# Which engine issues the stores of x: SyncE's queue or ScalarE's

## The chip, the cores and the metric

The kernel runs on one core of a Trainium2 chip. The metric is the time of one execution on the device, in microseconds (us). The engines are TensorE (PE; its weight loads are shown as PEld), VectorE (DVE), ScalarE (ACT), GpSimd (POOL) and SyncE (SP). Each has a queue of instructions that it works through in order; SP computes nothing and issues most of the DMA transfers.

## The reference

The program is attention followed by two mixtures of experts. All inputs are float32.

```
q, k, v: [4, 8, 576, 64]          # batch, heads, positions, head dim
out = upsample4(softmax_attention(mean4(q), mean4(k), mean4(v)))   # 144 pooled positions
    + softmax_attention(q, k, v, masked to |i - j| < 4)            # a local band
x  = out as rows [2304, 512]

# first mixture: 8 experts, two per row, the choice is made on noisy logits
logits = x @ w_gate + softplus(x @ w_noise) * noise
x  = sum over the two best e of  softmax weight * relu(x @ w1[e]) @ w2[e]      # w1 512x1024, w2 1024x512

# second mixture: 8 experts, one per row
logits = x @ w_gate2 + modality_bias[modality_id]
out = softmax probability of the best e * relu(x @ w1'[e]) @ w2'[e]
```

## The kernel before

**Attention.** The 32 heads are handled in pairs; one pair of one batch is a block, numbered 0 to 15, and two blocks make a group that shares its loads. The loop at L1114 is a software pipeline over the blocks: in one turn i it transposes q and k of block i+1, scores block i, and finishes the softmax, the transposes of the probabilities (`p_transposes`) and the product with v for blocks i−1 and i−2. The result of a batch lies transposed in `xT`.

**The rows x.** The 2304 rows are 18 tiles of 128 rows (t = 0 to 17). `xback_att(t)` turns a tile back to rows: PE multiplies pieces of xT with an identity that has the two routers' gate columns beside it (L971), into a PSUM tile px. What reads px is put off: a function `rest` is kept in the list `after`, and the next `flush()` runs it, so that PE isn't followed at once by work that waits for it. `rest` copies x from px to the SBUF tile `xr` on ACT (L987), sums the logits on DVE (L988) and stores xr into the DRAM rows `x_rows` (L989). xr has two buffers, so the copy of tile t must wait until the store of tile t−2 has landed. Tiles 0 to 12 are made inside the loop (the tables `before` and `behind` say in which turn); tiles 13 to 17 follow in a loop of their own (L1184), which I call the tail.

**Loads.** SP issues, in program order, the loads of q and k (`load_qk`, ten DMAs for a group), of v in two layouts (`load_vr`, two; `load_vw`, five), the small tables, two fills with zeros (`x_rows` beyond the 2304 rows at L1173; all of `x2_rows` at L1181), the routing weights `wb` (L1030), and the expert weights `raw` (L694 and L695, two DMAs of 512 KB for each). `ffn.begin` (L1176) issues the first two blocks of raw during turn 14, just ahead of the zeros of x2_rows; raw has three buffers, and the third block is loaded in the first step of `ffn.run`.

**Routing.** The first router's work (`route1`) is a generator. Its steps on DVE, POOL and PE are taken a few at a time between the instructions of attention (`tick`), from turn 12 on. When the places of the first tokens are known, POOL gathers their rows from x_rows (L720).

**Expert layers.** `FFN.run` goes through 20 items of up to 640 rows. An item's rows are gathered, transposed (L729), and multiplied in float32 split into a high and a low part (L746, L758); ACT and DVE split the weights (L706 to L709).

The order is written out by hand: the program is under a manual schedule, and each engine's queue has the instructions in the order of the code. The change touches L989 alone.

Of the kernel before, what the change touches and what calls it, by code (L numbers as in the profile page):

```python
# [871 lines left out]
def core(ctx, tc, q, k, v, moe_w_gate, moe_w_noise, moe_noise, moe_w1, moe_w2,  # L872
         moe2_modality_id, moe2_w_gate, moe2_modality_bias, moe2_w1, moe2_w2, out):
    nc = tc.nc
    B, H, S, D = q.shape
    DM = H * D
# [9 lines left out]
    x_rows = dram.tile([N + 640, XW], F32, tag="x_rows", name="x_rows")  # L886
# [28 lines left out]
    with ExitStack() as actx:  # L915
# [51 lines left out]
        def xback(t, halves):  # L967

            for o, b, s, n in pieces(t):
                for j in range(4):  # L970
                    nc.tensor.matmul(halves[j // 2][o:o + n, j % 2], att.xT[b][:, j, s:s + n], gw[:, j], start=True, stop=True)  # L971
            xr = axr.tile([128, 2, 2, 128], F32, tag="xr", name="xr")
            return xr
# [7 lines left out]
        def xback_att(t):  # L981
            px = att.psD.tile([128, 2, 512], F32, tag="D", name="px")
            pv = px[:, :, :2 * XB].rearrange("p a (b c) -> p a b c", b=2)
            xr = xback(t, [pv[:, 0], pv[:, 1]])

            def rest():
                nc.scalar.activation(xr, pv[:, :, :, :128], AF.Copy)  # L987
                nc.vector.tensor_reduce(lg[:, t], pv[:, :, :, 128:].rearrange("p a b c -> p c a b"), axis=AX.XY, op=ALU.add)  # L988
                nc.sync.dma_start(x_rows[128 * t:128 * t + 128, :DM], xr.rearrange("p a b c -> p (a b c)"))  # L989
            after.append(rest)  # L990

        def route1(c0, c1, bank, eng, heng, then=None):
# [203 lines left out]
    for i in range(5):  # L1196
        t = fpool.tile([128, YW], F32, tag=f"y{i}", name=f"y{i}")
# [473 lines left out]
```

## Time and profile before

Three runs took 926.56 to 929.01 us, with a median of 927.85. One more execution was profiled; the rows below come from it.

| | |
|---|---|
| profiled execution | 926.93 us |
| its span, first to last instruction | 925.2 us |
| PE busy | 870.4 us (94%) |
| DVE, ACT, POOL busy | 550.4, 429.0, 322.3 us |
| mean granted TensorE clock | 0.973 |
| stores of xr | 18 of 256 KB, all on SP |

How to read it: busy shares are averages over the stages. Attention lasts to about 178 us of the span, the expert layers from there to the end, and the two have different limits. DMA-issuing instructions aren't counted as busy time; in the timeline they stand under the queue's name (SPq), and their duration is the time until the queue can go on, not until the data has landed. A granted clock of 1.00 is 2.4 GHz, 0.50 is 1.2 GHz.

### The profile page before, as it was taken

To read this page: it belongs to the slowest core of one execution; us is meant where nothing else is said; L and a number is where in the kernel's file an instruction comes from. 1 tells how busy PE (TensorE), PEld (TensorE's weight loads), DVE (VectorE), ACT (ScalarE), POOL (GpSimd) and SP (SyncE) were. 2 spreads that over 40 slices of the span, in tenths; PEclk is the share of its full clock that TensorE was granted. 3 is DMA by queue.
4 is the path that set the end of the run, shared out by engine and by line. 5 is a ranking of instruction groups with operands and counts; after the bars stand their busy time and mean duration, and the time that the engine had idled before them with its cause. 6 is when DMAs were issued, how large, how long until landed. Compare 5 with 4: busy or idle time off the path is not lost. (4 is left out here: it accounts for less than half of the span.)

```text
span 925.2 us, 18236 instructions
## 1 busy us (share of the span) xinstructions
PE 870.4 (94%) x6775; PEld 764.1 (83%) x6775; DVE 550.4 (59%) x1345; ACT 429.0 (46%) x947; POOL 322.3 (35%) x460
## 2 busy tenths in 40 slices
PE   5898977799999999999999999989989999999995
PEld 4777866698888988999898999978867889999994
DVE  6775697489975544554343443434666877556662
ACT  3675644455554534444233342334423356455552
POOL 7876658436553213043106032050020442222210
PEclk9998988899999999999999999999989999999998
DMA  8878659747776457476328245175433467546650
GB/s 175 171 159 189 169 143 329 240 167 229 204 235 195 140 146 181 143 204 147 129 71 182 92 92 162 46 161 161 128 99 109 155 239 245 190 154 220 216 209 24
DMA packets 158702, 153.83 MB, mean 166 GB/s; under 512 B 74319, under 2 KB 119887, under 8 KB 158608
## 3 DMA queue, kind: packets, MB, share of 16 engines
q1 hardware_dynamic: 146528, 120.15, 42.2%
q0 software_dynamic: 12080, 32.45, 15.2%
q8 instruction: 56, 0.92, 0.4%
q14 instruction: 38, 0.31, 0.1%
HBM read 124.98 MB, written 27.85 MB: 165 GB/s over the span
## 5 line engine op out<-in xcount | busy, mean ns | idle before, releaser
L746 PE MATMUL ph<-xh,whi 128*128 128x256 f32 (+3 forms) x768 | 238.4, 310 | 2.8 <-DVE wlo L707 2.1
L746 PE MATMUL ph<-xl,whi 128*128 128x256 f32 (+3 forms) x768 | 237.6, 309 | 0.4 <-DVE xl L732 0.3
L746 PE MATMUL ph<-xh,wlo 128*128 128x256 f32 (+3 forms) x768 | 237.6, 309 | 0.1
L758 PE MATMUL y<-whi,hh 128*128 128x512 f32 x472 | 192.2, 407 | 0.1
L758 PE MATMUL y<-wlo,hh 128*128 128x512 f32 x472 | 188.1, 398 | 0.0
L758 PE MATMUL y<-whi,hl 128*128 128x512 f32 x472 | 187.6, 398 | 0.0
L707 DVE TENSOR_TENSOR wlo<-raw,whi 128x512 fp32r<-128x512 f32 x135 | 93.2, 690 | 157.4 <-ACT whi L706 144.9
L706 ACT ACTIVATE whi<-raw 128x512 fp32r<-128x512 f32 x160 | 101.0, 631 | 170.7 <-PE y L758 155.7
L746 PEld LDWEIGHTS ph<-xh,whi 128*128 128x128 f32 x768 | 146.0, 190 | 12.2 <-issue 2.6
L746 PEld LDWEIGHTS ph<-xl,whi 128*128 128x128 f32 x768 | 145.9, 190 | 8.3 <-DVE xl L732 1.0
L748 ACT ACTIVATE hh<-ph 128x256 fp32r<-128x256 f32 (+3 forms) x192 | 83.2, 433 | 142.3 <-PE ph L746 133.0
L746 PEld LDWEIGHTS ph<-xh,wlo 128*128 128x128 f32 x768 | 146.2, 190 | 1.8 <-DVE wlo L707 0.3
L749 DVE SCALAR_TENSOR_TENSOR hl<-ph,hh 128x256 fp32r<-128x256 f32 (+3 forms) x192 | 92.5, 482 | 84.5 <-ACT hh L748 81.0
L1215 POOL DMA_INDIRECT x_rows<-y,idx x35 | 57.4, 1641 | 208.1 <-ACT y L1206 108.2
L709 DVE TENSOR_TENSOR wlo<-raw,whi 128x512 fp32r<-128x512 f32 x160 | 120.6, 754 | 11.9 <-ACT whi L708 10.9
L758 PEld LDWEIGHTS y<-whi,hl 128*128 128x128 f32 x472 | 89.5, 190 | 21.6 <-DVE hl L749 0.4
L758 PEld LDWEIGHTS y<-whi,hh 128*128 128x128 f32 x472 | 90.2, 191 | 13.6 <-DVE y L1208 0.8
L758 PEld LDWEIGHTS y<-wlo,hh 128*128 128x128 f32 x472 | 89.8, 190 | 12.6
L708 ACT ACTIVATE whi<-raw 128x512 fp32r<-128x512 f32 x160 | 98.6, 616 | 0.0
L732 DVE TENSOR_TENSOR xl<-pt,xh 128x512 fp32r<-128x512 f32 x59 | 38.7, 687 | 30.8 <-ACT xh L731 30.6
L271 POOL TENSOR_TENSOR Pd<-pe,sm 32x380 f32<-32x380 f32 (+1 forms) x48 | 42.1, 877 | 42.8 <-ACT kT L198 10.4
L1215 POOL DMA_INDIRECT out_dram<-y,pi x19 | 20.6, 1084 | 100.6 <-ACT y L1206 44.1
(311 smaller groups left out, 1085.5 us busy)
## 6 DMA issues: line engine op xcount, KB each, us to landing
raw<-in_moe_w_dram SPq DMA_DIRECT2D x160, 512.0 KB
x_rows<-zero SPq DMA_DIRECT2D x1, 5934.0 KB
vr<-in_v_dram SPq DMA_DIRECT2D x16, 288.0 KB
x_rows<-xr SPq DMA_DIRECT2D x18, 256.0 KB
x2l<-x_rows SPq DMA_DIRECT2D x18, 256.0 KB
qk<-in_q_dram SPq DMA_DIRECT2D x32, 128.0 KB
qk<-in_k_dram SPq DMA_DIRECT2D x32, 128.0 KB
vw<-in_v_dram SPq DMA_DIRECT2D x24, 128.0 KB
```

The source lines that it names most:

```text
L271: eng.tensor_tensor(Pd[s, :, W * g:W * g + n], pe[s, :, :n], sm[s, :, None].to_broadcast([W, 2 * NB, n]), op=ALU.mult)
L706: nc.scalar.activation(h1, a, AF.Copy)
L707: eng.tensor_tensor(l1, a, h1.bitcast(F32), op=ALU.subtract)
L708: nc.scalar.activation(hi[:, 1], r2[:, half], AF.Copy)
L709: nc.vector.tensor_tensor(lo[:, 1], r2[:, half], hi[:, 1].bitcast(F32), op=ALU.subtract)
L732: nc.vector.tensor_tensor(xl, p, xh.bitcast(F32), op=ALU.subtract)
L746: nc.tensor.matmul(ps, w[a][:, k], x[b][:, k, s], start=(i == 0), stop=(i == 3 * KD - 1))
L748: nc.scalar.activation(hh[:, s], ps, AF.Relu)
L749: nc.vector.scalar_tensor_tensor(hl[:, s], ps, 0.0, hh[:, s].bitcast(F32), op0=ALU.max, op1=ALU.subtract)
L758: nc.tensor.matmul(p, h[a][:, 128 * j:128 * j + 128], w[b], start=(f == 0 and i == 0), stop=(f == self.FB - 1 and i == 2))
L1215: d = nc.gpsimd.indirect_dma_start(out=dst, out_offset=bass.IndirectOffsetOnAxis(ap=ix, axis=0), in_=y, in_offset=None, **kw)
```

## The change

The store of a tile of x is issued on ACT's queue, right behind ACT's copy into xr in program order (DVE's instruction between them is on another queue), in place of SP's queue. Shape, source, destination and the number of stores stay. All 18 tiles go through this function.

```diff
             def rest():
                 nc.scalar.activation(xr, pv[:, :, :, :128], AF.Copy)
                 nc.vector.tensor_reduce(lg[:, t], pv[:, :, :, 128:].rearrange("p a b c -> p c a b"), axis=AX.XY, op=ALU.add)
-                nc.sync.dma_start(x_rows[128 * t:128 * t + 128, :DM], xr.rearrange("p a b c -> p (a b c)"))
+                nc.scalar.dma_start(x_rows[128 * t:128 * t + 128, :DM], xr.rearrange("p a b c -> p (a b c)"))
             after.append(rest)
```

## Rows read from the trace of the kernel before

**Rows 1.** The page's first part: engine, busy us, share of the span, instructions.
```profile
PE 870.4 (94%) x6775; PEld 764.1 (83%) x6775; DVE 550.4 (59%) x1345; ACT 429.0 (46%) x947; POOL 322.3 (35%) x460
```

**Rows 2.** Windows by stage: stretch, length, busy us by engine, granted clock, DMA share, GB/s.
```profile
57.00:119.00 62.00, 57.00 (x1093) 49.34 (x1090) 41.85 (x113) 38.87 (x129) 41.55 (x54) 0.94 0.75 175
119.00:140.00 21.00, 14.72 (x196) 12.17 (x194) 20.45 (x64) 10.71 (x35) 9.43 (x13) 0.84 0.50 144
140.00:178.00 38.00, 28.92 (x413) 24.19 (x414) 25.11 (x88) 16.60 (x49) 27.73 (x46) 0.91 0.86 281
178.00:925.00 747.00, 726.98 (x4250) 642.87 (x4249) 424.09 (x985) 332.28 (x635) 200.66 (x267) 0.98 0.54 160
```

**Rows 3.** Timeline of PE: start, duration, line, operation, [idle before, releaser].
```profile
77.85 1.09 PE L285 MATMUL pp<-gw,Pd 128*128 128x128 f32 x8 [0.81 <-POOL Pd L271]
80.92 0.44 PE L285 MATMUL pp<-gw,Pd 128*128 128x128 f32 x2 [1.98 <-ACT pT L286]
...
153.59 1.73 PE L285 MATMUL pp<-gw,Pd 128*128 128x128 f32 x10
...
177.83 1.48 PE L729 MATMUL pt<-gw,xg 128*128 128x128 f32 x8 [3.09 <-DVE lg L988]
```

**Rows 4.** Tile xr, its stores: duration ns least/median/most, first and last start.
```profile
L989 SPq DMA_DIRECT2D x_rows<-xr x18: 320/350/9874, 64.9 to 177.5; - x18
```

**Rows 5.** Waits: us in total, times, longest; 50 to 185, last row 140 to 185.
```profile
DVE lg L988 <- ACT xr L987: 11.4, 7, 4.3
ACT xr L987 <- DMA x_rows<-xr: 8.2, 4, 4.3
...
ACT xr L987 <- DMA x_rows<-xr: 3.1, 2, 1.9
```

**Rows 6.** Timeline of SP's queue, 66 to 180.
```profile
74.02 0.83 SPq L989 DMA_DIRECT2D x_rows<-xr  x2
...
142.63 0.48 SPq L1181 DMA_DIRECT2D x_rows<-zero  x1
147.66 9.87 SPq L989 DMA_DIRECT2D x_rows<-xr  x1
157.64 0.40 SPq L1030 DMA_DIRECT2D x_rows<-wb  x1
158.13 6.33 SPq L989 DMA_DIRECT2D x_rows<-xr  x1
...
170.65 0.32 SPq L989 DMA_DIRECT2D x_rows<-xr  x1
...
177.92 0.43 SPq L694 DMA_DIRECT2D raw<-in_moe_w_dram  x1
```

**Rows 7.** Timeline of ACT, 66 to 190.
```profile
66.73 0.65 ACT L987 ACTIVATE xr<-px 128x512 f32<-128x512 f32 x1
...
79.80 0.60 ACT L987 ACTIVATE xr<-px 128x512 f32<-128x512 f32 x1 [4.25 <-DMA x_rows<-xr]
80.29 1.47 ACT L286 ACTIVATE pT<-pp 128x488 f32<-128x488 f32 x3
...
148.54 0.60 ACT L987 ACTIVATE xr<-px 128x512 f32<-128x512 f32 x1 [0.90 <-ACT xr L987]
154.76 1.31 ACT L286 ACTIVATE pT<-pp 128x488 f32<-128x488 f32 x3 [5.62 <-PE pp L285]
...
170.03 0.60 ACT L987 ACTIVATE xr<-px 128x512 f32<-128x512 f32 x1 [0.58 <-PE px L971]
...
189.97 0.63 ACT L706 ACTIVATE whi<-raw 128x512 fp32r<-128x512 f32 x1 [1.01 <-PE y L758]
```

**Rows 8.** Windows, columns as in rows 2.
```profile
84.00:85.00 1.00, 1.00 (x9) 0.67 (x9) 0.99 (x3) 1.00 (x7) 0.00 (x0) 0.50 1.16 261
...
154.00:156.00 2.00, 1.84 (x16) 1.49 (x15) 1.88 (x5) 1.24 (x4) 2.00 (x4) 0.88 1.08 382
...
168.00:170.00 2.00, 1.99 (x18) 1.57 (x13) 1.93 (x7) 0.60 (x1) 0.43 (x1) 1.00 0.04 12
```

## The prediction

> **What bounds the kernel now.** I read the engines' busy line first, then the same by stage. TensorE (PE) is busy for 870.4 of 925.2 us [rows 1]. By stage this splits in two [rows 2]: from 178 us on, in the expert layers, PE is busy 726.98 of 747 us, so a shift of the point where they start passes to the end one for one. In attention no engine is full: PE 57.00 of 62 us from 57 to 119, and 28.92 of 38 from 140 to 178, where ScalarE (ACT) has 16.60. That stage is a chain of hand-overs, and what a delay on ACT is worth must be read from the chain. The change lies there alone, so the time to forecast is where the expert layers start: today PE's first transposes of gathered rows at 177.83 [rows 3].
>
> The second thing to see is a spread: the 18 issues of this store by SyncE (SP) take 0.35 us at the median and 9.87 at the longest [rows 4]. The third is in the waits of attention: ACT's copies into xr wait 8.2 us, in 4 places, for a store that still holds the buffer (there are two), and VectorE (DVE) waits 11.4 us behind those copies [rows 5].
>
> **Removed: a stall of 4.25 us.** The store of tile 1 is issued at 74.02, because loads of q, k and v stand ahead of it in SP's queue; its copy had started at 66.73 and taken 0.65. The copy of tile 3, which needs that buffer again, starts at 79.80 after 4.25 us of idling; it could have started at 75.55 [rows 6, 7]. Issued by ACT, the store would go at 67.4. Landing took 79.80 − 74.02 = 5.8 us, so it would be down at 73.2, before 75.55. The stall goes. What is late next is PE: eight transposes of Pd take 1.09 us from 77.85, so the first four are there at 78.4 and the copies pT can start then instead of right behind the late copy at 80.29; PE's last two transposes, which waited 1.98 us for pT until 80.92, go 1.9 earlier [rows 3]. PE's granted clock is 0.50 in the row for 84 to 85, its lower level (1.2 GHz), after that idling; all six microseconds from 83 to 89 have it [rows 8]. At the upper level PE's work in them would be 3 us less, but DVE's and GpSimd's lies between; I take 0.6, with ends 0 and 2. Together **−2.5 us**, ends 0 and −4. Of the other three waits, 8.2 − 4.25 = 3.95 us, two with 3.1 lie in the tail after 170 [rows 5], and there SP issued 0.02 us behind the copy (170.65, for a copy from 170.03 to 170.63), so they stay. The third, 0.8, goes: **−0.5**, ends 0 and −0.9.
>
> **Added: ACT issues 18 stores.** Each waits for its own copy to end, so ACT's next instruction loses its overlap with the copy's tail (about 0.1 us, an estimate from 79.80 + 0.60 against the next start at 80.29), and then an issue follows: 0.32 to 0.50 us where SP's rows are undisturbed. Of the 18 copies 17 are followed by idle time on ACT, from 0.58 us (ahead of 170.03) to 5.62 (ahead of 154.76) [rows 7]; 0.45 us fits into each, so the cost is 0 and that idle time is the cover. The one without it (tile 3) gets one when the stall is gone. Without any cover it would be 18 × 0.45 = 8 us.
>
> **The price that decides.** At 142.63 SP issues the zeros of x2_rows, 5934 KB, in 0.48 us. Its next DMA, the store of tile 11, is held for 9.87 us, until 157.53. The weights wb (72 KB in pieces of 64 bytes) follow at 157.64 in 0.40, and the store of tile 12 is held 6.33 us, until 164.46 [rows 6]. Meanwhile the DMA engines are full (share 1.08, 382 GB/s; 0.04 by 168 to 170) [rows 8]. I read it so: an issue that follows a DMA of many pieces is held until that one has handed out its pieces. On SP this costs little, since behind the stores only the third weight block waits (177.92; ACT first uses it at 189.97). What the trace cannot show is whether ACT is held by SP's pieces, as no DMA is issued on ACT. The bounds for each of the two are 0.32, the shortest row of this store, and its hold on SP. I take the nearest rows: the very same two stores at the very same moments, with one thing different, the engine that issues. So ACT is held until 157.53 and 164.46.
>
> Queued on ACT behind store 11 is the copy of tile 12 (148.54 becomes 157.6), on which DVE's reduction and all of DVE's later work waits; behind store 12 are the copies pT of block 15, which start at 154.76 [rows 7] and would at 164.5: **+9.7 us**. The 5.62 us of idling ahead of them are no cover past 154.76, as PE's transposes for them began at 153.59 [rows 3]. From there to the end of the tail the order is pT, exp, softmax, Pd on GpSimd, PE, pT, values, xT, px, the copies of tiles 13 to 17, with each engine's other work in the same program order; I absorb nothing. If half of that chain had slack it would be +5; if PE comes back at the lower clock, +11.
>
> The Trainium skill, DMA: Bandwidth & Descriptors, section Queues, rings and completion order, speaks for this: ScalarE and SyncE own a row of rings each, but no descriptor generator of their own. By it alone the store on ACT meets the same hold, and the term is +9.7. The same page, section Issuing engines are not separate DMA queues, points the other way: issuing from several engines saves issue time only, which is usually small; by it the hold is SP's own and the term is 0. SP's rows agree with neither in full: an issue took 9.87 us here, which isn't small, and which engine such a hold binds no run here shows.
>
> **Moved past.** SP no longer waits for copies, so the loads behind the stores come earlier. The waits from 50 to 185 name no load that was late, so in attention that gains 0. The third weight block (1 MB) goes once wb is handed out, about 165, and the fourth when its buffer is free, after the second split. That one runs beside the last stores and the first gathers: 1 MB at 382 GB/s is 2.7 us of the DMA engines, spread over 8 us with a mean share of 0.86 in the stage [rows 2]. +0.5 taken, ends 0 and 1.5. It saves nothing later, since ACT didn't wait for it.
>
> **Sum.** −2.5 − 0.5 + 9.7 + 0.5 = +7.2 us. The profiled execution took 926.93 us (span 925.2 and 1.7 around it); the median of the three runs is 927.85, 0.92 more. 926.93 + 7.2 = 934.1, on the median's footing 935.0; I say 934.5.
>
> **Rivals.** (1) Nothing of SP's holds ACT: its store goes out in 0.32 to 0.50 us and shares the DMA engines with the zeros. Then −2.5 − 0.5 + 0.5 = −2.5, 925 us; with the clock's far end 923. For it: the zeros' own issue took 0.48 us although most of their pieces were still to come, so what keeps pieces waiting isn't the engine that issued them. Against: the next issue was held all the same, and nothing in the rows ties the hold to SP. It decides at 157.5: is pT of block 15 begun by then, about 1 us behind PE's L285, or not. (2) ACT's first store is taken in without a hold and lands late, and only the second is held, until 157.53: pT starts at 157.6, +2.8, and the sum is +0.3, 927.7. For it: behind the store of tile 11 wb was taken in within 0.40 us. Against: the store right behind the zeros was not. (3) The stall is removed, but its gain is lost between 119 and 140, where DVE is busy 20.45 of 21 us [rows 2]. Against: what DVE does there hangs on the blocks before it, so it should shift along. By it the forecast becomes +10, 937.5, and rival 1 is 928.
>
> **How the numbers follow.** Forecast 0.45, rival 1 0.37, rival 2 0.11, rival 3 0.07. A measurement of this kernel can tell about 0.3% (2.8 us) from no change. Rival 1 lies near that bound: 0.6 of it faster, 0.37 the same. Faster: 0.37 × 0.6 + 0.11 × 0.15 + 0.01 = 0.25. The same: 0.37 × 0.37 + 0.11 × 0.65 + 0.45 × 0.07 + 0.04 = 0.28. Slower: the rest, 0.47. The range reaches from rival 1 with its clock, 922.5, to the upper side of the forecast, 938.5; the forecast's own range is 930 to 939.
>
> **What would show it.** The stall: ACT's copy of tile 3 waits under 1 us, and the granted clock stays at 1.00 over the next 8 us. The hold: in ACT's queue an issue of x_rows<-xr lasts over 5 us near 148 and again near 158, and pT of block 15 starts 9 to 10 us behind PE's transposes. The tail: PE's first transposes of gathered rows come at about 185 (at 175 by rival 1), and what follows keeps its length. If all 18 issues on ACT stay below 1 us, the prediction is wrong and rival 1 is right.

## The result and the profile after

| | before | after |
|---|---|---|
| median | 927.85 us (7 runs, 924.87 to 929.01) | 931.91 us (7 runs, 929.22 to 934.59) |
| profiled execution's span | 925.2 us | 930.1 us |
| mean granted TensorE clock | 0.973 | 0.970 |

The ratio is 1.0053, with a 95% interval of 1.0032 to 1.0074. So the change costs about half a per cent. The time lies in the range given and on the side forecast, but not by the mechanism forecast: ACT is held nowhere, and two other losses stand in its place.

First the store itself, in the view of its line in the kernel after (queue, duration in ns least/median/most, first and last start), to be read against [rows 4], and the entry of the page's list of DMA queues that is new (packets, MB, share):

```profile
L989 ACTq DMA_DIRECT2D x_rows<-xr x18: 326/327/393, 61.8 to 184.6; - x18
```

```profile
q10 hardware_dynamic: 2592, 4.72, 1.4%
```

All 18 issues take 0.33 to 0.39 us where SP's longest took 9.87. The stores have a queue of their own, q10 (4.72 MB, which is 18 times 256 KB). Next, ACT's timeline after (start, duration, [idle before, releaser]), for [rows 7]:

```profile
68.71 0.62 ACT L987 ACTIVATE xr<-px 128x512 f32<-128x512 f32 x1
69.36 0.35 ACTq L989 DMA_DIRECT2D x_rows<-xr  x1
...
71.01 0.33 ACTq L989 DMA_DIRECT2D x_rows<-xr  x1
...
77.34 0.64 ACT L987 ACTIVATE xr<-px 128x512 f32<-128x512 f32 x1
...
151.08 0.33 ACTq L989 DMA_DIRECT2D x_rows<-xr  x1
...
152.53 0.33 ACTq L989 DMA_DIRECT2D x_rows<-xr  x1
158.12 1.31 ACT L286 ACTIVATE pT<-pp 128x488 f32<-128x488 f32 x3 [5.62 <-PE pp L285]
...
177.53 0.60 ACT L987 ACTIVATE xr<-px 128x512 f32<-128x512 f32 x1 [0.98 <-DMA x_rows<-xr]
...
183.97 0.60 ACT L987 ACTIVATE xr<-px 128x512 f32<-128x512 f32 x1 [5.85 <-DMA x_rows<-xr]
```

The copy of tile 3, at 77.34, no longer waits; pT of block 15 has the same 5.62 us of idling ahead of it as before; and the copy of tile 17 now waits 5.85 us. And SP's timeline after, for [rows 6]:

```profile
72.31 0.37 SPq L131 DMA_DIRECT2D qk<-in_q_dram  x1
...
75.65 0.37 SPq L131 DMA_DIRECT2D qk<-in_k_dram  x1
...
81.53 0.88 SPq L144 DMA_DIRECT2D vr<-in_v_dram  x2
...
142.20 0.51 SPq L1181 DMA_DIRECT2D x_rows<-zero  x1
154.90 4.36 SPq L1030 DMA_DIRECT2D x_rows<-wb  x1
159.31 6.00 SPq L694 DMA_DIRECT2D raw<-in_moe_w_dram  x1
...
174.50 0.37 SPq L694 DMA_DIRECT2D raw<-in_moe_w_dram  x1
```

ACT issued at 151.08 and 152.53 in 0.33 us each. SP's wb, the DMA next behind the zeros on SP, was issued later than these, at 154.90, and was still held until 159.26. So the hold binds the queue of the DMA with the many pieces, not the other one. The third block of raw is already issued at 159.31 and the fourth at 174.50 (before, the third block's first DMA came at 177.92). In the waits of SP's queue from 56 to 145 (total us, times, longest) there are rows for x_rows<-xr that the kernel before doesn't have; the two large ones are:

```profile
SPq L158 <- DMA x_rows<-xr: 14.1, 2, 7.1
...
SPq L131 <- DMA x_rows<-xr: 7.4, 4, 3.5
```

SP's loads of q and k (L131) and of v (L158) wait for stores that ACT issued, which write other memory. Why stands in the built program. Every DMA that SP or ACT issues raises one of eight completion semaphores, given out in turn over both engines, and waits until the DMA eight places ahead has landed. The instructions around the loads of the third group, in that order:

```
place  issued by   what                            semaphore   waits for
 80    ACT         store of tile 1                 7           place 72
 83    ACT         store of tile 2                 2           place 75
 88    SP          first load of q (L131)          7           place 80: store of tile 1
 91    SP          second load of k (L131)         2           place 83: store of tile 2
102    SP          a load of vw (L158)             5           place 94: store of tile 3
```

With all of them on SP's queue, no row of the kernel before shows SP waiting for a store in this way. With the stores on ACT the DMA eight places ahead is one that another engine issued lately: the store of tile 1 goes out at 69.36, and SP's load at place 88 only at 72.31; the store of tile 2 at 71.01, place 91 at 75.65. The load of vr, 81.53 here, went out at 73.04 in the kernel before:

```profile
73.04 0.88 SPq L144 DMA_DIRECT2D vr<-in_v_dram  x2
```

What waits for it, in the timelines of POOL and PE after, for [rows 3]:

```profile
86.02 0.72 POOL L183 TENSOR_TENSOR vd<-vr 72x256 f32<-72x256 f32 x1 [5.01 <-DMA vr<-in_v_dram]
```

```profile
92.22 2.39 PE L285 MATMUL pp<-gw,Pd 128*128 128x128 f32 x10 [5.57 <-POOL Pd L271]
...
184.88 1.97 PE L729 MATMUL pt<-gw,xg 128*128 128x128 f32 x8 [6.78 <-DVE lg L988]
```

POOL's next Pd is queued behind vd, and PE waits 5.57 us for Pd. Windows of the kernel after, columns as in [rows 2, 8]:

```profile
84.00:85.00 1.00, 1.00 (x20) 0.77 (x16) 0.93 (x4) 1.00 (x6) 0.00 (x0) 1.00 0.84 214
90.00:96.00 6.00, 3.78 (x20) 3.55 (x21) 0.00 (x0) 2.36 (x7) 5.61 (x10) 0.50 0.91 190
```

The lower clock (1.2 GHz) has moved: 84 to 85 runs at 2.4 GHz now, and 90 to 96, behind the new idling, at 1.2.

The account between the two profiled executions goes by the same instruction in both: ACT's copies kT of the transposed keys (L198, one for each block), the copy of tile 13 into xr, then PE's L729. The copies kT around the stall and the late loads, before and after:

```profile
74.27 0.62 ACT L198 ACTIVATE kT<-pk 128x512 f32<-128x512 f32 x1
...
85.28 0.62 ACT L198 ACTIVATE kT<-pk 128x512 f32<-128x512 f32 x1
...
94.52 0.60 ACT L198 ACTIVATE kT<-pk 128x512 f32<-128x512 f32 x1
```

```profile
76.22 0.62 ACT L198 ACTIVATE kT<-pk 128x512 f32<-128x512 f32 x1
...
84.45 0.64 ACT L198 ACTIVATE kT<-pk 128x512 f32<-128x512 f32 x1
...
98.77 0.60 ACT L198 ACTIVATE kT<-pk 128x512 f32<-128x512 f32 x1 [1.28 <-PE pk L195]
```

- +1.95 us up to the kT of 74.27. Of this +1.80 is there at the kT of 57.74, before the first store, so it is the execution's own. Between the two SP's load of vw (L158, 65.42) waits 7.1 us for the store of tile 0; that costs at most the 0.15 left.
- −2.78 over the stall: 74.27 to 85.28 took 11.01, now 76.22 to 84.45, 8.23.
- +5.08 over the late loads: 85.28 to 94.52 took 9.24, now 84.45 to 98.77, 14.32.
- −0.84 from there to the copy of tile 13 (168.85, now 172.26).
- +3.64 in the tail, from that copy to PE's L729: 8.98, now 12.62.
- −2.15 from L729 to the end: 747.4, now 745.2.

The sum is +4.90, as the spans. The last term can't be put down to the change: from L729 to the end the twelve other profiled kernels here took 743.0 to 748.9 us. The stretches before it vary less from one execution to another. In the kernel before and the experiments below with two buffers, the stall's stretch took 10.78 to 11.62 us and that of the loads 8.97 to 9.24 where all of attention's stores stay on SP, and the tail 8.70 to 8.98 where its own stores do.

### The profile page after: what moved, and what is told of

The parts are those of the page before. It is cut to its first block, busy times and chain, and to the rows that moved or that the text cites. A ratio compares the mean times of both kernels' runs of the same rounds, so it can differ in the third digit from the quotient of the medians.

```text
span 930.1 us, 18203 instructions
## 1 busy us (share of the span) xinstructions
PE 868.5 (93%) x6775; PEld 762.8 (82%) x6775; DVE 550.2 (59%) x1345; ACT 428.9 (46%) x947; POOL 321.8 (35%) x460
## 3 DMA queue, kind: packets, MB, share of 16 engines
q10 hardware_dynamic: 2592, 4.72, 1.4%
```

## The experiments

The two losses are far apart in the program, so the change can be cut in two. The first kernel moves the stores of tiles 0 to 12 alone, the second those of 13 to 17.

```diff
-                nc.sync.dma_start(x_rows[...], xr...)
+                (nc.scalar if t < 13 else nc.sync).dma_start(x_rows[...], xr...)
```

> Tiles 0 to 12 (inside the loop over the blocks) are stored by ACT, tiles 13 to 17 (the tail) by SP as before. My theory: in the built program the DMAs of SP and ACT take eight completion semaphores in turn, and a DMA waits for the one eight places ahead of it; so SP's loads of q, k and v wait for ACT's stores to land. The stall of tile 3 goes (-2.8 us between the kT copies at 74 and 85), v comes late for GpSimd in the next block (+5), and the tail is as before: 929.5 us, 927.5 to 932, with rows of SP that wait for x_rows<-xr. Rival, the whole loss is in the tail, where the third and fourth weight blocks run beside the last stores: then this kernel has only the gain, 924.5.

Measured: 930.04 us, ratio 1.0027 (1.0011 to 1.0042). SP's waits for the stores and PE's first transposes of gathered rows:

```profile
SPq L158 <- DMA x_rows<-xr: 13.3, 2, 6.7
...
SPq L131 <- DMA x_rows<-xr: 6.8, 4, 3.5
```

```profile
182.90 1.76 PE L729 MATMUL pt<-gw,xg 128*128 128x128 f32 x8 [2.81 <-DVE lg L988]
```

The waits of SP are those of the whole change: the stretch of the late loads takes 15.02 us, that of the stall 8.23. The tail is as before (8.70 us from the copy of tile 13, at 174.20). The loss in attention exists by itself.

```diff
-                nc.sync.dma_start(x_rows[...], xr...)
+                (nc.scalar if t >= 13 else nc.sync).dma_start(x_rows[...], xr...)
```

> Tiles 13 to 17 are stored by ACT, 0 to 12 by SP as before. My theory: attention up to 168 us is as before, stall of tile 3 included; SP is free after wb, the third and fourth weight blocks are loaded beside the last stores and gathers, the copy of tile 17 waits 4 to 6 us for a landing, PE's first transposes of gathered rows come 3 to 4 us later than at 177.83, and the expert layers give back about 2 us: 929.4 us, 927.5 to 931. Rival: the tail is harmless (its wait is noise of the one profiled execution) and the time is 927.9, the wait under 2 us.

Measured: 930.21 us, 1.0033 (1.0015 to 1.0051). ACT's copy of tile 17 in this kernel:

```profile
182.56 0.60 ACT L987 ACTIVATE xr<-px 128x512 f32<-128x512 f32 x1 [4.81 <-DMA x_rows<-xr]
```

The stall at tile 3 is there as before (4.89 us), SP waits for no store, and the tail's loss is there: 11.73 us from the copy of tile 13 to PE's L729. The halves add up within their intervals: 0.27% and 0.33% against 0.53% for the whole.

Next, the stall that the change removes can be removed without another queue: a third buffer for xr, all stores on SP.

```diff
-    axr = xctx.enter_context(tc.tile_pool(name="axr", bufs=2, side="right"))
+    axr = xctx.enter_context(tc.tile_pool(name="axr", bufs=3, side="right"))
```

> The kernel before, stores on SP, with three buffers of xr in place of two. Theory: the copies' waits for a landing (8.2 us in 4 places) go without any new one, since no store leaves SP's queue: -2.8 at tile 3, and up to -3 in the tail: 923 us, 921.5 to 925.5. Rival: the waits in the tail are replaced by that for the gathered rows, -2.8 only, 925; or nothing of it is on the path, 927.9.

Measured: 920.5 us, 0.9916 (0.9899 to 0.9933); run once more with the last group below, 920.48, 0.9914 (0.9893 to 0.9935). No copy of ACT waits for a store, in attention or in the tail, and SP has no wait for one. It is ahead of both kernels, and by more than the 923 expected. In its trace the stall's stretch takes 8.24 us, that of the loads 8.38 and the tail 6.83, together 5.8 less than before; the rest of the 7.7 us isn't accounted for.

Then one store alone, that of tile 1, on ACT, with two buffers. If the landing of stores makes SP wait, one is enough.

```diff
-                nc.sync.dma_start(x_rows[...], xr...)
+                (nc.scalar if t == 1 else nc.sync).dma_start(x_rows[...], xr...)
```

> Only the store of tile 1 is issued by ACT, 17 stay on SP. Theory (shared completion semaphores): the first load of q of the next group on SP has the same semaphore as this store eight places earlier and waits until it has landed, 3 to 4 us; the stall of tile 3 is gone (-2.8), but the loads behind (q, k, v) start about 4 us later, and GpSimd waits for v in the following block (up to +5): 927 to 931 us, with a row of SP's L131 that waits for x_rows<-xr. Rival (the loads are late because 18 stores on a second queue take a larger share of the DMA engines): a single store changes nothing but the stall, 925 us, and SP's loads go out at 66 to 67 as before.

Measured: 928.5 us, 1.0004 (0.9989 to 1.0019). SP's wait and its timeline:

```profile
SPq L131 <- DMA x_rows<-xr: 3.5, 1, 3.5
```

```profile
73.21 0.38 SPq L131 DMA_DIRECT2D qk<-in_q_dram  x1
...
79.62 0.89 SPq L144 DMA_DIRECT2D vr<-in_v_dram  x2
```

The copy of tile 3 doesn't stall (78.80, no wait), and still nothing is won: the group's first load waits 3.5 us, and what the stall gave back goes there. The stretch of the stall takes 8.08 us (2.93 less than before), that of the loads behind it 12.32 (3.08 more).

Third buffer and change together:

```diff
-    axr = xctx.enter_context(tc.tile_pool(name="axr", bufs=2, side="right"))
+    axr = xctx.enter_context(tc.tile_pool(name="axr", bufs=3, side="right"))
...
-                nc.sync.dma_start(x_rows[...], xr...)
+                nc.scalar.dma_start(x_rows[...], xr...)
```

> The change as it stands (all 18 stores issued by ACT), with xr given a third buffer. Base: the kernel before with a third buffer ran 920.5. Theory (two separate losses: SP's loads in attention wait for stores to land; in the tail the copies wait for the stores' landing because raw blocks move beside them): the third buffer takes the landing waits of the copies away in the tail (no ACT xr <- DMA row over 1 us), but not the waits of SP's loads of q, k and v behind x_rows<-xr (10 us or more in all, as in the changed kernel), so PE still waits for Pd behind vr in the third group: 920.5 + 4 = about 924.5, 923 to 926.5. Rival (the changed kernel loses only through its two buffers): no loss against three buffers on SP, 920.5, and no waits of SP for x_rows<-xr.

Measured: 928.41 us, 1.0017 (1.0001 to 1.0032), 4 us more than the theory's number. SP's waits (50 to 185), PE's first transposes, and POOL:

```profile
SPq L158 <- DMA x_rows<-xr: 13.3, 3, 6.6
...
SPq L131 <- DMA x_rows<-xr: 7.3, 4, 3.1
```

```profile
180.31 0.66 PE L729 MATMUL pt<-gw,xg 128*128 128x128 f32 x4 [0.95 <-DVE lg L988]
...
182.92 0.66 PE L729 MATMUL pt<-gw,xg 128*128 128x128 f32 x4 [1.96 <-DMA xg<-x_rows,idx]
```

```profile
182.93 0.20 POOL L805 COPY meta<-xg 128x16 f32<-128x16 f32 x1 [4.50 <-DMA xg<-x_rows,idx]
```

The rival is wrong: the buffers don't cure the loads, whose stretch takes 13.83 us (8.38 with three buffers and all stores on SP). The theory is right on them and on the copies, none of which waits for a landing, but not on the tail. PE's first four transposes come on time, 6.79 us behind the copy of tile 13. The next four wait for a gather xg that lands late: POOL waits 4.50 us for it here, 4.30 in the changed kernel and 2.29 before. So two buffers were one way in which the tail's loss showed, not its source. What the profile has against before is the moment of the raw blocks (157.55 and 175.76 here), beside the last stores and the gathers.

That moment can be tested by itself. With tiles 13 to 16 on ACT and tile 17 on SP, SP's queue, and the raw blocks in it, stands behind the copy of tile 17 again.

```diff
-                nc.sync.dma_start(x_rows[...], xr...)
+                (nc.scalar if 13 <= t < 17 else nc.sync).dma_start(x_rows[...], xr...)
```

> Two buffers; stores of tiles 13 to 16 on ACT, tiles 0 to 12 and tile 17 on SP. So SP's queue, and with it the third and fourth block of raw, stands behind the copy of tile 17 as before. Theory (the tail's loss is raw blocks loaded early, beside the last stores): no loss, 927.5 to 929, the waits of the last two copies at most 2 us, third block of raw issued at the tail's end. Rival (stores issued on ACT's queue land later by themselves): loss as with tiles 13 to 17 on ACT, about 930.2, and a wait of 4 to 6 us at the copy of tile 17 or 16.

Measured: 928.56 us, 1.0010 (0.9994 to 1.0027). ACT's copy of tile 17, and SP:

```profile
177.72 0.60 ACT L987 ACTIVATE xr<-px 128x512 f32<-128x512 f32 x1 [1.96 <-DMA x_rows<-xr]
```

```profile
178.72 0.43 SPq L694 DMA_DIRECT2D raw<-in_moe_w_dram  x1
```

Four of the five stores on ACT, and the copy waits 1.96 us in place of 4.81; the tail takes 8.73 us, as before. The store that this copy waits for, that of tile 15, is issued by ACT in both kernels, at 174.21 here and at 176.05 in the kernel with all five on ACT, where the fourth block of raw goes out at 173.98. So ACT's queue is not what makes a store land late; the raw blocks beside it are. (By the times alone a small loss isn't excluded: the interval reaches from no loss to 0.27%.)

Does a third buffer cure the tail where only its stores are on ACT?

```diff
-    axr = xctx.enter_context(tc.tile_pool(name="axr", bufs=2, side="right"))
+    axr = xctx.enter_context(tc.tile_pool(name="axr", bufs=3, side="right"))
...
-                nc.sync.dma_start(x_rows[...], xr...)
+                (nc.scalar if t >= 13 else nc.sync).dma_start(x_rows[...], xr...)
```

> Three buffers for xr, stores of tiles 0 to 12 on SP, 13 to 17 on ACT. Raw blocks load early beside the last stores, as with the same tiles on ACT and two buffers (930.2, 2 to 3 us over before). Theory (the loss in the tail is the copy's wait for the landing of the store two tiles back): with a buffer more the copy of tile 17 waits for the store of tile 14, which landed long ago, so the loss goes: 920.5, 919.5 to 921.5, PE's first transposes of gathered rows within 1 us of those of three buffers on SP (174.9). Rival (the early raw blocks delay the last store itself and the gathers behind it): 922 to 923.5, no wait at the copies, but PE's first transposes 2 us or more later.

Measured: 928.96 us, 1.0022 (1.0004 to 1.0040), against both expectations. ACT's timeline:

```profile
172.69 0.60 ACT L987 ACTIVATE xr<-px 128x512 f32<-128x512 f32 x1 [2.15 <-DMA x_rows<-xr]
...
179.28 0.60 ACT L987 ACTIVATE xr<-px 128x512 f32<-128x512 f32 x1 [5.99 <-DMA x_rows<-xr]
...
183.47 0.60 ACT L987 ACTIVATE xr<-px 128x512 f32<-128x512 f32 x1 [2.53 <-DMA x_rows<-xr]
```

With three buffers a copy should wait for the store three tiles back. In the built program it doesn't: the copy of tile 14 waits for the store of tile 13, that of 15 for 14, that of 17 for 15, because the build put the stores of tiles 11 and 12, late on SP, behind those of 13 and 14 on ACT in its order of DMAs. So the copies of tiles 14 and 15 had in effect one buffer. Nor did all of raw load early: the second halves of the third and fourth block go out only at 172.62 and 183.40. The kernel says nothing on the question.

The last four isolate the wait for the semaphore. Three buffers, all stores on SP, and one DMA more that nothing reads: 512 bytes of tile 1, written to a scratch place behind the copy of tile 1. First issued by ACT, as 128 pieces of 4 bytes:

```diff
+        scr = dram.tile([128, 1], F32, tag="scr", name="scr")
...
+                if t == 1:
+                    nc.scalar.dma_start(scr, xr[:, 0, 0, :1])
                 nc.sync.dma_start(x_rows[...], xr...)
```

> Three buffers for xr, all stores on SP, and one more DMA added: ACT writes 512 bytes (one float of each of 128 rows) of tile 1 to a scratch place in DRAM, behind its copy of tile 1. No store is moved. Theory (the HWDGE DMAs of SP and ACT take eight completion semaphores in turn, and a DMA waits until the one eight places ahead has landed): one DMA more on ACT shifts the turns, and loads of SP's next group stand behind ACT's DMA: a wait of SP at the loads of q, k (L131) or v for that DMA's landing, 2 to 4 us, vr later by as much, POOL waits for vr: 922 to 925 against 920.5. Rival (what hurts is the 256 KB of a store beside the loads): 512 bytes cost nothing: 920.5 within 1 us, no wait of SP.

Measured: 929.98 us, 1.0027 (1.0011 to 1.0043). SP's wait, the load that waited, and a window (columns as in [rows 2]):

```profile
SPq L131 <- DMA scr<-xr: 10.8, 1, 10.8
```

```profile
78.02 0.38 SPq L131 DMA_DIRECT2D qk<-in_q_dram  x1
```

```profile
72.00:74.00 2.00, 2.00 (x30) 1.81 (x23) 1.13 (x3) 0.66 (x2) 1.93 (x3) 1.00 0.00 0
```

512 bytes undo all of the third buffer's gain. ACT issued them at 70.17. SP, which had issued the store of tile 0 at 66.72, issues its next DMA, a load of q, only at 78.02. The theory is right on what waits for what and was too low on the size: SP's load stands for 10.8 us for a DMA that it shares nothing with but the semaphore, while the DMA engines are idle (share 0.00).

The same 512 bytes issued by GpSimd, whose DMAs are outside the eight semaphores:

```diff
-                    nc.scalar.dma_start(scr, xr[:, 0, 0, :1])
+                    nc.gpsimd.dma_start(scr, xr[:, 0, 0, :1])
```

> Three buffers, all stores on SP, and the same extra DMA (one float of each of 128 rows of tile 1 to a scratch place), issued by GpSimd in place of ScalarE. In the built program GpSimd's DMAs don't count in the eight semaphores that SP's and ACT's share. Theory (the shared semaphores make SP wait): SP waits for nothing of scr, the loads of q of the third group start where they do without it (within 1 us of the store of tile 0), 920 to 921.5, at most 1 us for the issue on POOL, which idles 2.85 us ahead of 77.80. Rival (128 writes of 4 bytes clog the DMA engines for the loads, whoever issues them): 925 to 930, as with the same DMA on ACT, and vr late by 5 us or more.

with, for comparison in the same group of runs,

> The kernel before with a third buffer for xr once more, beside the two small DMAs of this group, so that they are compared within one group of runs. Both theories: as before, ratio about 0.9916, some 920; the first load of q (L131) of the third group goes out within 1 us of the store of tile 0 on SP.

Measured: 927.08 us, 0.9990 (0.9974 to 1.0006), against 0.9914 without it. SP's timeline (L992 is the store), and a window:

```profile
65.19 0.38 SPq L992 DMA_DIRECT2D x_rows<-xr  x1
65.66 1.43 SPq L131 DMA_DIRECT2D qk<-in_q_dram  x1
```

```profile
78.00:80.00 2.00, 0.66 (x4) 0.53 (x5) 0.00 (x0) 0.00 (x0) 1.79 (x2) 1.00 0.40 36
```

SP doesn't wait, as the theory has it, and the time is the rival's. GpSimd issued at 71.59, and from 76 to 82 all transfers crawl (36 to 76 GB/s; 218 and 265 from 76 to 80 without the extra DMA). PE stands for 3.25 us from 79.4 with nothing named as its releaser. So 128 pieces of 4 bytes seem to be a disturbance of their own, and the kernel before this one had them too. So once more with the 512 bytes in one piece, first by ACT:

```diff
-                    nc.scalar.dma_start(scr, xr[:, 0, 0, :1])
+                    nc.scalar.dma_start(scr, xr[:1, 0, 0, :])
```

> Three buffers, all stores on SP, and the extra DMA on ACT again, with the same 512 bytes in one piece (one row of tile 1). Its place in the turn of the semaphores is the same: the first load of q of the third group waits for it. Theory (what counts is when the DMA of ACT has landed): the 128 pieces landed 7.8 us after their issue at 70.17; one piece lands in about 2 us, so SP goes on at about 72.2 in place of 78.0 and 67.4 without it: a wait of 4 to 6 us at L131, vr at about 80, and 923 to 926 of 920. Rival (the pieces did it): no loss, 920 to 921, no wait of SP.

Measured: 923.93 us, 0.9956 (0.9936 to 0.9976).

```profile
SPq L131 <- DMA scr<-xr: 4.4, 1, 4.4
```

```profile
70.68 0.47 ACTq L991 DMA_DIRECT2D scr<-xr  x1
```

```profile
71.81 0.38 SPq L131 DMA_DIRECT2D qk<-in_q_dram  x1
```

As the theory has it, in wait, moment and time: SP goes on 1.1 us after ACT's issue, which comes late because it follows the copy. And the one piece by GpSimd:

> Three buffers, all stores on SP, and the extra 512 bytes in one piece (one row of tile 1) issued by GpSimd, whose DMAs don't count in the eight semaphores of SP and ACT; the same piece issued by ACT gave 0.9956 of before, no extra DMA 0.9914, and 128 pieces issued by GpSimd 0.9990 with the DMA engines at 36 to 76 GB/s from 76 to 82 us. Theory (ACT's piece cost only through SP's wait for its landing, GpSimd's 128 pieces only through the pieces): no wait of SP for scr, the first load of q of the third group within 1 us of the store of tile 0, ratio 0.990 to 0.993, 920 to 921.5. Rival (any extra DMA at this place shifts the order of the loads and costs): 0.995 or more, 923.5 or more.

Measured: 923.14 us, 0.9944 (0.9924 to 0.9965). SP's timeline:

```profile
67.38 0.38 SPq L992 DMA_DIRECT2D x_rows<-xr  x1
67.86 0.38 SPq L131 DMA_DIRECT2D qk<-in_q_dram  x1
```

SP doesn't wait, and the profiled execution (918.89 us) is as the theory expects, but the timed ones are not: the interval overlaps both that of the piece on ACT and that of no extra DMA. So the wait itself is shown to come from ACT's place in the turn, but the times don't separate what one such wait of 4.4 us costs from the cost of an extra DMA. The traces do, if only by one execution each: the stretch of the loads takes 8.39 us without the extra DMA, 8.38 with the piece issued by GpSimd, and 10.11 with the piece issued by ACT, so the wait costs 1.7 us there. The pieces count too: 128 of them by GpSimd gave 0.9990 where one gave 0.9944, and their intervals don't overlap.

## Why the prediction came out as it did

**Removed: a stall of 4.25 us.** Right: −2.78 measured, −2.5 said; the clock in 84 to 85 is back at 2.4 GHz. The small third wait, −0.5 said, fits the −0.65 between the kT of 112.87 and that of 123.66.

**ACT issues 18 stores.** Right: 0.33 us each, 0 on the path. In the two stretches from kT to kT behind the late loads, each with two stores and no copy that waits for one, ACT's issues add nothing: 9.84 and 8.39 us, where they took 9.91 and 8.44.

**The price that decides.** Wrong, and this is the step that failed: +9.7 was said, 0 measured. SP's two rows showed a hold, and I gave it to the store; it belongs to the queue that holds the DMA with the many pieces. ACT issued in 0.33 us at 151.08, before the hold on SP's queue ended at 159.26, and pT of block 15 came with the very same 5.62 us of idling. The nearest rows were the same store at the same moment, but the one thing that differed, the queue, was what decided. The Trainium skill (DMA: Bandwidth & Descriptors, Queues, rings and completion order) says that ScalarE and SyncE have no descriptor generator of their own; whatever they share, this trace shows no hold across the two.

**Moved past.** Wrong on both sides. In attention the premise failed: the loads behind the stores did not come earlier but later. "In attention that gains 0" looked only for loads that had been late; it measured +5.08, since SP's loads now waited for ACT's stores. That wait shows in no row of before. The tail's +0.5 measured +3.64: the early raw blocks weren't paid for with 2.7 us of the engines spread over 8, but fell on the last stores, whose landing the copies with two buffers wait for (0.98 and 5.85 us where there were 1.27 and 1.88).

**The rivals.** Rival 1's mechanism was right (no hold), its time, 925, was not, as it took over the step "moved past". Rivals 2 and 3 are out: no store was held, and the stall's gain wasn't lost between 119 and 140 (the kT of 123.66 to the next takes 12.15 us in both) but before, at 86 to 98. So the side and the time came out right by luck: two losses that I had at +0.5 together came to about +8.7 and took the place of one that I had at +9.7.

**Still open.** What in the raw blocks' transfers keeps the last stores and gathers, bandwidth or the order of the queues, wasn't separated; nor what slowed all transfers after GpSimd's 128 pieces, which one trace shows.

## What to carry to other kernels

Before a DMA is moved to another engine, look in the built program at what its completion semaphore is shared with: DMAs behind it in the turn, on other engines, may come to wait for its landing. Where a copy waits for its buffer's store, try another buffer before another queue: here that gave 0.8% where the queue cost 0.5%. And a queue that a store has blocked is also a schedule: freed, its next loads come early and fall on whatever runs then.

## What the runs showed of the hardware that was not expected

The hold behind the zeros bound only the queue that had issued them: SP's next DMA, issued at 154.90, was held for 4.36 us, while ACT's, issued before that at 151.08 and 152.53, went out in 0.33 us each. In the other two kernels that store tiles 0 to 12 or all tiles through ACT, no issue on ACT took over 0.40 us. 512 bytes in 128 pieces of 4 bytes let SP go on 7.85 us after their issue (70.17 to 78.02), in one piece 1.13 us (70.68 to 71.81). Issued by GpSimd at 71.59, the 128 pieces were followed, from 76 to 82, by six microseconds in which the DMA engines moved 36 to 76 GB/s at a busy share of 0.40 to 0.90.
